# The first norm of a four-layer attention kernel: one tile's statistics and the root on ScalarE, masked queries taken from PSUM

## The chip, the cores and the metric

The kernel runs on one core of a Trainium2 chip. Five engines work side by side: TensorE (PE; PEld is its weight load), VectorE (DVE), ScalarE (ACT), GpSimd (POOL) and SyncE (SP), which issues the DMAs. The metric is the device time of one launch in microseconds, lower is better.

## The reference

Four layers work on one sequence of 2048 tokens with 512 features: A, B, A, B, with the same weights for both A layers and for both B layers. Cut to what matters:

```python
x = A_x                                                  # 1 x 2048 x 512, bf16
x = x + A(layernorm(x));  x = x + B(layernorm(x))
x = x + A(layernorm(x));  x = x + B(layernorm(x))

def layernorm(x):                                        # over the 512 features
    return (x - mean(x)) / sqrt(var(x) + 1e-5)

def A(x):       # 32 heads of 16, 4 segments of 512 tokens, one after the other
    q, k, v = heads(x @ wq), heads(x @ wk), heads(x @ wv)
    for s in segments:
        a_dot = softmax(q[s] @ k[s].T / 4 + causal_mask) @ v[s]     # inside the segment
        a_mem = phi(q[s]) @ M / (phi(q[s]) @ z + 1e-6)              # memory of earlier segments
        out[s] = g * a_mem + (1 - g) * a_dot                        # g = sigmoid(beta), per head
        M += phi(k[s]).T @ v[s];  z += sum(phi(k[s]))
    return out @ wo

def B(x): return softmax(q @ k.T / 4) @ v @ wo           # 32 heads over all 2048 tokens
```

## The kernel before

The program is written out once, at build time, by a planner in Python (`Builder`), and every engine then runs its own fixed list in order. The planner keeps an estimated time for each engine (the `ns` and `gap` arguments); it picks from a list of attention units and a list of background tasks (norm, projections, memory, output) and appends the instructions. What waits for what follows from the tiles that each instruction reads and writes, and is kept by semaphores: an instruction waits for the last writer of what it reads. Two rules matter here. A PSUM bank counts as one tile, and where two engines read the same bank, the later reader in the program also waits for the earlier one (`last_read_any` in `Sched.add`). And a bank that is to be written anew waits for all who read its old content.

**The attention unit.** Attention works in units of up to three banks of scores: three matmuls of 32 rows (one for each head of a group, from the masked queries `qm` and the keys `KA` or `KB`), one exponential on ScalarE over the three banks (L1349), and later the product with the values. The units use the banks 0 to 2 and 4 to 6 in turn, bank 3 (`DXB`) takes the background's matmuls once attention runs, and bank 7 (`ACC`) collects the product with the values. Queries are masked because a group holds every second head: `qm` is a copy of the 128 query rows in which the other heads' rows are multiplied by zero (`par` holds the mask; L1266, one instruction for each half of the heads).

**The start.** Everything before the first unit is one chain, and the change lies there:

- `setup` (L447 on) issues the loads on SP's queue: the first four tiles of x, one by one (128 tokens each), then the weights wk, wq, wv, beta, then the other twelve tiles of x in three loads, then wo, wqkv and wo of B. PE runs 66 matmuls on an identity meanwhile. DVE reduces the head mask to `par` and sets two PSUM banks, `ACC` and `DXB`, to zero (L490).
- `task_A` for layer 0, segment 0, calls `ln_part`: per tile `bn_stats` (L519) and `bn_aggr` (L521) on DVE, then 1 / sqrt(var + eps) for the four tiles at once by eight small instructions on DVE (L526 to L533: a first value from the bits of the number, and two Newton steps).
- `ln_first` normalizes the four tiles on DVE (L552), transposes them on PE (L406, 16 matmuls) into banks 3 and 0, and copies them to `xT`: the first half on ACT, the second on DVE (L564, L565).
- Then the projections of the first 128 features: keys into bank 1, copied to `KA` by DVE (L429), queries into bank 2, copied to `QA` by ACT (L427); DVE masks `QA` twice into `qm` (L1266); the first three score matmuls write banks 0 to 2; the projection of the values follows behind them in PE's list, and the first exponential waits for all three.

From there on, background and attention interleave to the end of the program.

## Time and profile before

| | before |
|---|---|
| median of 3 runs | 1893.77 us (1893.45 to 1894.54) |
| the profiled execution: own time | 1894.24 us |
| its span, first to last instruction | 1892.7 us |
| granted TensorE clock, mean | 0.994 |
| busy: PE, ACT, DVE, POOL | 89%, 95%, 81%, 15% of the span |
| first exponential of attention starts | 14.48 us |

The profiled execution took 1.54 us more than its span (what lies before the first and behind the last instruction), and 0.47 us more than the median of the runs. All times of the trace count from the first instruction of the span.

In the profile's rows a line number is that of the kernel's source; "out<-in" names the tiles; "xN" merges N instructions in a row on one engine, with the time that they cover together; the bracket tells how long the engine stood idle and what ended that.

### The profile page before, as it was taken

What the parts mean: (1) busy time and instruction counts of PE and PEld (TensorE: products, weight loads), DVE (VectorE), ACT (ScalarE), POOL (GpSimd) and SP (SyncE); (2) the same over time, 40 slices, a digit from 0 to 9 for tenths busy, and PEclk for the clock granted to TensorE, in tenths of its full rate; (3) what the DMA queues carried; (4) which work ended last, traced back from release to release, by engine and by line L of the source; (5) the groups of instructions that cost most, each with busy time, mean ns of one, the idle gap of its engine ahead of it and who ended that gap; (6) DMA issues with size and microseconds to landing.
All of it is one profiled execution on the core that took longest, in us unless ns stands there. A gap on an engine that the chain in (4) does not pass through costs nothing.

```text
span 1892.7 us, 64181 instructions
## 1 busy us (share of the span) xinstructions
PE 1686.8 (89%) x27966; PEld 891.0 (47%) x28200; DVE 1535.3 (81%) x3230; ACT 1798.6 (95%) x1642; POOL 277.7 (15%) x646
## 2 busy tenths in 40 slices
PE   7879888899998999999989989899888898889887
PEld 4444445566665556665656656555522222222222
DVE  6566657698797678797778779678999999999996
ACT  6899999899999999999999999999999999999998
POOL 4522333010001110001110050420100000000000
PEclk9999999999999999999999999999999999999999
DMA  5121110000000002000001011010100000000000
GB/s 159 29 35 38 24 18 19 14 14 17 14 8 9 8 8 31 12 19 8 9 8 33 11 24 25 19 19 3 14 12 1 1 11 2 2 1 13 1 1 12
DMA packets 94971, 33.51 MB, mean 18 GB/s; under 512 B 87521, under 2 KB 94177, under 8 KB 94689
## 3 DMA queue, kind: packets, MB, share of 16 engines
q1 hardware_dynamic: 94688, 29.39, 8.0%
q8 instruction: 221, 3.62, 0.8%
q14 instruction: 62, 0.50, 0.1%
HBM read 6.30 MB, written 2.10 MB: 4 GB/s over the span
## 4 chain that ended last, share of the span: by engine, by line
PE 40%; ACT 29%; DVE 16%; issue 12%; DMA 2%; POOL 1%; SPq 0%; ACTq 0%; DVEq 0%; POOLq 0%
PE ps L402 40%; ACT pT L1349 29%; DVE dxw L980 3%; DVE dxw L1032 2%; DMA xT<-xn 1%; DVE ob L1459 1%; DVE lnst L519 1%; DVE x L795 1%; POOL pT L1364 1%; DVE QA L980 0%; DVE rd L1447 0%; DVE VA L1032 0%; DVE wA L980 0%; DVE KB L980 0%; DVE QA L1032 0%
## 5 line engine op out<-in xcount | busy, mean ns | idle before, releaser
L1349 ACT ACTIVATE pT<-ps 128x1536 bf16<-128x1536 f32 (+3 forms) x1605 | 1771.4, 1249 | 70.4 <-PE ps L402 57.6
L402 PE MATMUL ps<-qm,KB 32*128 32x512 bf16 x3584 | 491.6, 386 | 79.5 <-ACT pT L1349 56.5
L1364 POOL TENSOR_SCALAR_AFFINE_SELECT pT<-pT 128x256 bf16<-128x256 bf16 (+2 forms) x529 | 212.8, 421 | 830.4 <-ACT pT L1349 821.0
L402 PEld LDWEIGHTS ps<-VB,pT 128*128 128x128 bf16 x7800 | 256.6, 96 | 162.2 <-issue 107.0
L402 PE MATMUL ps<-VB,pT 128*128 128x51 bf16 (+1 forms) x7800 | 321.9, 187 | 10.7 <-DVE ob L1459 5.5
L980 DVE TENSOR_SCALAR dxw<-ps 128x512 uint16<-128x512 f32 (+1 forms) x309 | 269.8, 876 | 48.9 <-PE ps L402 45.6
L402 PEld LDWEIGHTS ps<-qm,KB 32*128 32x128 bf16 x3584 | 122.2, 91 | 284.0 <-ACT pT L1349 195.2
L402 PE MATMUL ps<-VB,dxw 128*128 128x34 bf16 (+1 forms) x5112 | 212.9, 186 | 0.2 <-issue 0.2
L1032 DVE TENSOR_SCALAR dxw<-dxw 128x1024 uint16<-128x1024 uint16 (+1 forms) x401 | 164.5, 426 | 8.0 <-PE ps L402 5.3
L402 PEld LDWEIGHTS ps<-VB,dxw 128*128 128x128 bf16 x5112 | 167.6, 96 | 5.7 <-issue 3.6
L1266 POOL TENSOR_SCALAR qm<-QB,par 128x512 bf16<-128x512 bf16 x74 | 57.9, 785 | 688.9 <-PE ps L402 560.3
L402 PE MATMUL ps<-VA,pT 128*128 128x51 bf16 (+1 forms) x3036 | 126.7, 188 | 20.0 <-DVE ob L1459 12.6
L402 PEld LDWEIGHTS ps<-VA,pT 128*128 128x128 bf16 x3036 | 100.0, 96 | 77.9 <-POOL pT L1364 42.8
L402 PE MATMUL ps<-qm,KA 32*128 32x128 bf16 (+3 forms) x1024 | 106.1, 303 | 24.0 <-ACT pT L1349 16.1
L402 PE MATMUL ps<-pT,VB 128*17 128x512 bf16 x791 | 126.1, 384 | 1.5 <-DVE KA L1477 0.6
L402 PE MATMUL ps<-qm,QA 32*128 32x512 bf16 x512 | 89.6, 385 | 24.8 <-ACT pT L1349 21.7
L402 PE MATMUL ps<-dxw,VB 128*17 128x512 bf16 x313 | 86.4, 381 | 0.0
L402 PEld LDWEIGHTS ps<-qm,KA 32*128 32x128 bf16 x1024 | 30.5, 91 | 87.7 <-ACT pT L1349 60.9
L402 PE MATMUL ps<-xT,wB 128*128 128x512 bf16 x223 | 63.4, 388 | 5.2 <-issue 2.4
L402 PE MATMUL ps<-xT,wA 128*128 128x512 bf16 x217 | 59.6, 380 | 8.4 <-issue 3.5
L402 PEld LDWEIGHTS ps<-pT,VB 128*17 128x17 bf16 x791 | 29.8, 87 | 76.4 <-issue 66.6
L402 PE MATMUL ps<-wB,zero 128*128 128x512 bf16 x173 | 60.9, 392 | 3.6 <-issue 2.4
(293 smaller groups left out, 2378.8 us busy)
## 6 DMA issues: line engine op xcount, KB each, us to landing
out_dram<-x SPq DMA_DIRECT2D x8, 256.0 KB, 2.1
x<-in_A_x_dram SPq DMA_DIRECT2D x3, 512.0 KB, 9.6
wB<-in_B_wqkv_dram SPq DMA_DIRECT2D x1, 1536.0 KB, 11.8
xT<-xn SPq DMA_TRANSPOSE x60, 2.5
oT<-ob SPq DMA_TRANSPOSE x52, 2.4
x<-in_A_x_dram SPq DMA_DIRECT2D x4, 128.0 KB, 2.1
wA<-in_A_wk_dram SPq DMA_DIRECT2D x1, 512.0 KB, 5.3
wA<-in_A_wq_dram SPq DMA_DIRECT2D x1, 512.0 KB, 6.2
```

The costliest lines, as they stand in the source:

```text
L402: self.sc.add("pe", lambda e: e.matmul(out, lhsT, rhs, start=start, stop=stop, skip_group_check=True), reads=reads, banks=[(bank, "w", all ...
L519: self.op("dve", (lambda i, t: lambda e: e.bn_stats(st[:, k, i, 0:6], self.x[:, t, :]))(i, t), reads=[self.b_x[t]], writes=[bs], ns=690)
L795: self.op("dve", (lambda t, o: lambda e: e.tensor_tensor(self.x[:, t, :], self.x[:, t, :], o, ALU.add))(t, o), reads=[self.b_x[t]], writes ...
L980: self.sc.add("dve", lambda e: e.tensor_scalar(d, o, SCALE * LOG2E * 128, EXP_C, op0=ALU.mult, op1=ALU.add), writes=[w for j in range(k) f ...
L1032: self.op("dve", lambda e: e.tensor_scalar(o, w, d, None, op0=ALU.add), reads=self.b_dxw[b0][:len(ents)], writes=wr, ns=435 if len(ents) = ...
L1266: self.op(eng, (lambda m, q, col: lambda e: e.tensor_scalar(m, q, col, 0.0, op0=ALU.mult, op1=ALU.add))(m, q, col), reads=[bq, self.b_par] ...
L1349: self.sc.add("act", (lambda dst, src: lambda e: e.activation(dst, src, ACT.Exp, scale=SCALE))(dst, src), writes=self.b_pT[slot * 3 + i:sl ...
L1364: self.op("pool", (lambda blk, pat: lambda e: e.affine_select(blk, blk, pattern=pat, compare_op=ALU.is_ge, fill=0.0, base=0, channel_multi ...
L1459: self.op("dve", lambda e: e.tensor_tensor(ob, src[:, :, 0:16], rb, ALU.mult), reads=[br] + bsrc, writes=[self.b_ob[oi][g.e]], bank=bk, al ...
```

## The change

Six edits, all in what runs before the first exponential or is queued there:

- **Statistics.** For the first segment `ln_part` is replaced by `ln_start`. Tiles 0, 1 and 3 keep `bn_stats` and `bn_aggr` on DVE. Tile 2 goes to ACT: a Copy with an accumulated sum gives minus the scaled mean, a Square with that as its bias and an accumulated sum gives the variance; DVE turns the first into the mean with one small instruction.
- **Root.** ACT takes sqrt(var + eps) of the four tiles in one Sqrt, and DVE one reciprocal, in place of the eight small instructions. Sqrt and Exp belong to different activation tables; a one-element Exp behind the Sqrt brings the second table back. In ACT's list there are now three table loads: ahead of the Copy, ahead of the Sqrt, ahead of that Exp.
- **Memsets.** `DXB` is no longer zeroed, and `ACC` is zeroed behind the four normalizing instructions in DVE's list instead of ahead of the statistics.
- **Masked queries from PSUM.** `first_heads` projects the queries first (bank 1), then the keys (bank 2). DVE writes the first masked queries straight from PSUM; ACT copies the queries to `QA` behind it (same bank, so it waits for the mask). The second mask is still made from `QA`.
- **First keys apart.** DVE copies keys 0 to 127 from bank 2, ACT the other 384 behind that; the first score matmuls wait for the small copy alone as far as the keys go.
- **Loads.** wq is loaded ahead of wk, and the load of tiles 4 to 7 of x waits on SP until wq and wk have landed; the loads behind it in SP's queue (the rest of x, wo, wqkv, wo of B) stand behind that wait.

In the compiled lists PE's instructions are the same in number and kind and in the same order; the other engines' lists differ only in the instructions named here.

```diff
@@ setup
-        for a, b in [...]: ... writes=self.b_x[a:b])
+        ... writes=self.b_x[a:b], deps=[self.b_wA[i].last_write for i in (0, 1)] if a == 4 else [])
             if a == 3:
-                for i, nm in ((1, "A_wk"), (0, "A_wq"), (2, "A_wv")):
+                for i, nm in ((0, "A_wq"), (1, "A_wk"), (2, "A_wv")):
...
-        for bk in (ACC, DXB):
-            ...
-            self.op("dve", (lambda b: lambda e: e.memset(self.ps[:, b.col0:b.col0 + 512], 0.0))(b), bank=b, alloc=-1)
+        pool(lambda e: e.memset(self.eps[:, :], LN_EPS), [self.b_eps])
@@ new
+    def ln_start(self):
+        junk, root = self.pT[:, 0, 0, :], 512 ** 0.5
+        for i in (0, 1, 3):
+            ... bn_stats, bn_aggr of x[:, i, :] on dve
+        nb = st[:, k, 2, 0:1]
+        self.op("act", lambda e: e.activation(junk, self.x[:, 2, :], ACT.Copy, scale=-1 / (512 * root), accum_out=nb), ...)
+        self.op("act", lambda e: e.activation(junk, self.x[:, 2, :], ACT.Square, scale=1 / root, bias=nb, accum_out=st[:, k, 2, 7:8]), ...)
+        self.op("dve", lambda e: e.tensor_scalar(st[:, k, 2, 6:7], nb, -root, None, op0=ALU.mult), ...)
+        self.op("act", lambda e: e.activation(v, var, ACT.Sqrt, bias=self.eps[:, 0:1]), ...)
+        self.op("act", lambda e: e.activation(self.eps[:, 1:2], self.eps[:, 0:1], ACT.Exp), ...)
+        self.op("dve", lambda e: e.reciprocal(y, v), ...)
@@ ln_first, behind the four normalizing instructions
+        self.op("dve", lambda e: e.memset(self.ps[:, b.col0:b.col0 + 512], 0.0), bank=b, alloc=-1)     # ACC
@@ new, in place of proj_fm of keys and queries for layer 0, segment 0, c = 0
+    def first_heads(self, slot):
+        for i, dst in ((0, self.QA), (1, self.KA)):
+            bank, al = self.misc(), self.new_alloc()
+            ... four matmuls into the bank
+            if i:
+                dve: tensor_copy(d[:, 0:128], o[:, 0:128]), writes b_K0
+                act: activation(d[:, 128:512], o[:, 128:512], ACT.Copy), reads b_K0
+            else:
+                dve: tensor_scalar(qm[:, 0, :], o, par[:, 0:1], 0.0, op0=ALU.mult, op1=ALU.add)
+                act: activation(d, o, ACT.Copy)
@@ select
+                if (g.L, g.qseg, g.c, g.e) == (0, 0, 0, 0):
+                    self.sel.append(g)
+                    continue                       # its mask was made in first_heads
@@ unit
-                kt = lambda kb: (..., self.b_KA[sl][g.c])
+                kt = lambda kb: (..., self.b_K0 if (g.L, g.qseg, g.c, kb) == (0, 0, 0, 0) else self.b_KA[sl][g.c])
```

More of the change, by code (lines that the diff above doesn't have):

```diff
@@ L314, in alloc @@
         self.lnw = sb("lnw", [P, 2, 4, 4], f32)
+        self.eps, self.b_eps = sb("eps", [P, 2], f32), Buf("eps")
+        self.b_K0 = Buf("k0")
         self.bet = sb("bet", [P, H], bf)
@@ L534, in ln_part @@
         return k
+    def ln_start(self):
+        k = self.ring("ln", 2)
+        st, w = self.lnst, self.lnw
+        bs = self.b_lnst[k]
+        junk, root = self.pT[:, 0, 0, :], 512 ** 0.5
+        yield [], 0, 3000
+        for i in (0, 1, 3):
+            self.op("dve", (lambda i: lambda e: e.bn_stats(st[:, k, i, 0:6], self.x[:, i, :]))(i), reads=[self.b_x[i]], writes=[bs[i]], ns=690)
+            self.op("dve", (lambda i: lambda e: e.bn_aggr(st[:, k, i, 6:8], st[:, k, i, 0:6]))(i), reads=[bs[i]], writes=[bs[i]], ns=180)
+        nb = st[:, k, 2, 0:1]
+        self.op("act", lambda e: e.activation(junk, self.x[:, 2, :], ACT.Copy, scale=-1 / (512 * root), accum_out=nb),
+                reads=[self.b_x[2]], writes=[bs[2], self.b_pT[0]], ns=620, gap=500)
+        self.op("act", lambda e: e.activation(junk, self.x[:, 2, :], ACT.Square, scale=1 / root, bias=nb, accum_out=st[:, k, 2, 7:8]),
+                reads=[self.b_x[2], bs[2]], writes=[bs[2], self.b_pT[0]], ns=620, gap=500)
+        bw = self.b_lnw[k]
+        v, y, var = w[:, k, 0, :], w[:, k, 1, :], st[:, k, :, 7]
+        self.op("dve", lambda e: e.tensor_scalar(st[:, k, 2, 6:7], nb, -root, None, op0=ALU.mult), reads=[bs[2]], writes=[bs[2]], ns=165)
+        self.op("act", lambda e: e.activation(v, var, ACT.Sqrt, bias=self.eps[:, 0:1]), reads=bs + [self.b_eps], writes=[bw], ns=230, gap=150)
+        self.op("act", lambda e: e.activation(self.eps[:, 1:2], self.eps[:, 0:1], ACT.Exp), reads=[self.b_eps], writes=[self.b_eps], ns=1500,
+                gap=1400)
+        self.op("dve", lambda e: e.reciprocal(y, v), reads=[bw], writes=[bw], ns=165)
+        return k
     def normalize(self, s, k, i):
@@ L554, in ln_first @@
                     reads=[self.b_x[t], self.b_lnst[k][t], self.b_lnw[k]], writes=[bx])
+        b = self.banks[ACC]
+        b.alloc = -1
+        self.op("dve", lambda e: e.memset(self.ps[:, b.col0:b.col0 + 512], 0.0), bank=b, alloc=-1)
         for j in range(2):
@@ L625, in task_A @@
         yield need, 0, 0
-        k = yield from self.ln_part(L, s)
+        k = yield from (self.ln_part(L, s) if L or s else self.ln_start())
         yield ["xT"], 0, 0
@@ L1308, in unit @@
                 sl = self.aslot(g.L, g.qseg)
-                kt = lambda kb: (self.KA[rows, sl, g.c, kb * 128:(kb + 1) * 128], self.b_KA[sl][g.c])
+                kt = lambda kb: (self.KA[rows, sl, g.c, kb * 128:(kb + 1) * 128], self.b_K0 if (g.L, g.qseg, g.c, kb) == (0, 0, 0, 0) else self.b_KA[sl][g.c])
                 parts = PARTS[what]
```

30 lines of the change are left out of this document (23 added, 7 removed).

## The prediction

> **What bounds the kernel now.** I read the page's busy shares first, then the chain of waits over the stretch that the change touches, then the timeline of that stretch, and last the rows that give prices. Over the whole program ScalarE is the fullest engine:
>
> ```profile
> PE 1686.8 (89%) x27966; PEld 891.0 (47%) x28200; DVE 1535.3 (81%) x3230; ACT 1798.6 (95%) x1642; POOL 277.7 (15%) x646
> ```
>
> That average says nothing of the first 14 us, where ScalarE does almost nothing. What counts there is the chain (start, us, what), here from the end of the head mask to the first exponential:
>
> ```profile
> by line: DVE lnst L519 19.5%; PE ps L402 17.4%; PE ps L406 11.6%; issue 8.3%; DVE ps L490 8.2%; DVE lnst L521 6.2%; DVE xT L565 5.9%; ACT QA L427 5.1%; DVE xn L552 3.5%; DVE qm L1266 3.1%; DVE lnw L532 2.9%; DVE lnw L531 2.9%; DVE lnw L533
> ```
>
> Memsets (L490), statistics (L519, L521) and root (lnw) all stand on the path, and so do the query copy and the mask. No DMA does. So what is saved here moves the first exponential, and with it everything behind it, as long as nothing later hangs on an absolute time. The timeline gives the places (start, length, engine, instruction):
>
> ```profile
> 0.80 1.82 SPq L449 DMA_DIRECT2D x<-in_A_x_dram  x4
> 0.80 1.28 ACT L564 ACT_TABLE_LOAD   x1 [0.80 <-PEq L1697]
> 2.57 1.03 DVE L490 MEMSET ps<- 128x512 f32 x2
> 3.50 0.64 DVE L519 BATCH_NORM_STATS2 lnst<-x 128x6 f32<-128x512 bf16 x1
> ...
> 5.86 0.66 DVE L519 BATCH_NORM_STATS2 lnst<-x 128x6 f32<-128x512 bf16 x1
> 6.56 0.18 DVE L521 BATCH_NORM_AGGREGATE lnst<-lnst 128x2 f32<-128x6 f32 x1
> 6.77 0.17 DVE L526 TENSOR_SCALAR lnw<-lnst 128x4 f32<-128x4 f32 x1
> ...
> 8.17 0.16 DVE L533 SCALAR_TENSOR_TENSOR lnw<-lnw 128x4 f32<-128x4 f32 x1
> 8.37 0.73 DVE L552 TENSOR_SCALAR xn<-x,lnst,lnw 128x512 bf16<-128x512 bf16 x2
> 9.02 0.73 DVE L552 TENSOR_SCALAR oT<-x,lnst,lnw 128x512 bf16<-128x512 bf16 x2
> 9.59 1.02 ACT L564 ACTIVATE xT<-ps 128x1024 bf16<-128x1024 bf16 x1 [7.51 <-PE ps L406]
> 10.24 0.69 DVE L565 COPY xT<-ps 128x1024 bf16<-128x1024 bf16 x1 [0.49 <-PE ps L406]
> 12.14 0.69 DVE L429 CAST KA<-ps 128x512 bf16<-128x512 f32 x1 [1.21 <-PE ps L402]
> 13.00 0.60 ACT L427 ACTIVATE QA<-ps 128x512 bf16<-128x512 f32 x1 [2.39 <-PE ps L402]
> 13.63 0.62 DVE L1266 TENSOR_SCALAR qm<-QA,par 128x512 bf16<-128x512 bf16 x2 [0.80 <-ACT QA L427]
> 14.04 0.39 PE L402 MATMUL ps<-qm,KA 32*128 32x512 bf16 x3 [1.08 <-DVE qm L1266]
> 14.36 1.04 PE L402 MATMUL ps<-wA,xT 128*128 128x512 bf16 x4
> 14.48 2.79 ACT L1349 ACTIVATE pT<-ps 128x1536 bf16<-128x1536 f32 x2 [0.88 <-PE ps L402]
> 17.16 0.23 ACT L496 ACTIVATE gtok<-bet 128x32 f32<-128x32 bf16 x1
> 17.27 0.23 ACT L496 ACTIVATE gout<-bet 128x32 f32<-128x32 bf16 x1
> ```
>
> To be seen: DVE works without a break from 2.57 to the end of the normalizing at 9.75, the eight root instructions alone take 6.77 to 8.33, and three places count: normalizing starts at 8.37, the transposed x is whole at 10.93, the score matmuls start at 14.04, which is 3.11 behind 10.93.
>
> Rows for prices, from the page (landing of a load behind its issue, median) and from the groups (count, busy, mean ns):
>
> ```profile
> x<-in_A_x_dram SPq DMA_DIRECT2D x4, 128.0 KB, 2.1
> wA<-in_A_wk_dram SPq DMA_DIRECT2D x1, 512.0 KB, 5.3
> wA<-in_A_wq_dram SPq DMA_DIRECT2D x1, 512.0 KB, 6.2
> ```
>
> ```profile
> L1349 ACT ACTIVATE pT<-ps 128x512 bf16<-128x512 f32 x91 | 50.7, 671 | 4.8 <-PE ps L402 3.5 <-POOL pT L1364 0.8
> L1349 ACT ACTIVATE pT<-ps 128x256 bf16<-128x256 f32 x48 | 19.8, 412 | 0.1
> L1435 DVE COPY KB<-ps 128x272 f32<-128x272 f32 x8 | 3.4, 430 | 0.5 <-PE ps L402 0.5
> L1447 DVE RECIPROCAL rd<-ps 128x16 f32<-128x16 f32 x88 | 22.0, 250 | 42.9 <-PE ps L402 42.3
> ```
>
> **Part 1: statistics and root, to the start of normalizing.** Without the memsets DVE waits for the first tile, issued at 0.80 and landed 2.1 later, at 2.90. Its three tiles then take 0.79 each (5.86 against 3.50 is three steps) and end at about 2.95 + 3 x 0.79 = 5.3. That is not what comes last. ScalarE's branch does: the third tile is issued 0.93 behind the first (four issues cover 1.82), so at 1.73, and lands at 3.83, work begins at about 3.90. Copy 0.60 (the QA row, same size); reading out the sum is not in the trace, I take the shortest ScalarE instruction, 0.23, in full, since the next step waits for it; hand-over 0.03; Square 0.60; read-out 0.23; table load 1.28 with 0.04 around it; Sqrt 0.23; hand-over 0.03; reciprocal 0.20 (between the 0.17 of a four-element DVE instruction and the 0.25 of L1447); hand-over 0.03. Sum 3.50, so normalizing starts at 7.40 against 8.37: **0.97 gained**. The small mean instruction on DVE waits for the Square and lies beside the table load. Bounds: with free read-outs (0.46 less) and a 0.17 reciprocal the gain is 1.46; with 0.67 for each 512-wide pass (the L1349 row) and a 0.35 reciprocal it is 0.68.
>
> The Trainium skill, "ScalarE: Activation LUTs", section "What ACT_TABLE_LOAD costs", adds about 93 ns for a per-partition pointer operand, which the Square and the Sqrt each carry as a bias. By it the sum of part 1 would be about 0.78; no row of this trace shows such an operand on ScalarE.
>
> **Part 2: from normalizing to the transposed x.** The same instructions, plus the `ACC` memset, 0.49 (two in 1.03), that now stands between the normalizing and DVE's half of the copy. In the trace DVE idles exactly 0.49 there, waiting for PE. So it fits with nothing to spare, and costs 0.05, between 0 and 0.10. ScalarE's half must be free for the other half: behind the Sqrt, which ends 0.26 before normalizing starts, come a table load and the small Exp, 1.28 + 0.02 + 0.23, so it is free 1.27 behind the start of normalizing, and PE's first half is ready 1.22 behind it (9.59 against 8.37). Its copy ends 1.27 + 1.02 = 2.29 behind, DVE's half 2.56 + 0.05. The second table load is hidden by 0.3 and costs nothing. The transposed x is whole at 10.93 - 0.97 + 0.05 = 10.01.
>
> **Part 3: from there (X) to the score matmuls.** The queries are in PSUM at X + 1.21 (12.14 against 10.93). DVE's mask from PSUM costs what such a pass costs, 0.69: X + 1.90. ScalarE's copy of the queries reads the same bank and waits for it: X + 1.93 to X + 2.53. The keys are in PSUM at X + 2.07 (13.00); DVE's 128 columns cost 0.32 (between 0.25 for 16 and 0.43 for 272): X + 2.40. The first score matmul can start there, 0.7 earlier than now. But the three write banks 0, 1 and 2, which now hold nothing, queries, keys. The second waits for ScalarE's query copy, the third for ScalarE's copy of the other 384 key columns, which stands behind the query copy in ScalarE's list. It costs 0.51 (between 0.41 for 256 and 0.60 for 512) and overlaps its forerunner by 0.11 (the two gate rows, 0.23 long and 0.12 apart): X + 2.42 to X + 2.95, and the third matmul starts at X + 3.00 against X + 3.11. The first exponential needs all three, and the value projection stands behind the third in PE's list. So masking from PSUM and the split copy together give **0.1**, not 0.7: ScalarE's two copies in a row are late next. Bounds: 0, without the overlap, and 0.15.
>
> **Part 4: loads.** wq, now first, lands where wk did, 2.67 + 5.3 = 7.97, wk where wq did, 3.15 + 6.2 = 9.35. Queries start at X + 0.1 = 10.1 and keys 0.86 later: neither waits. Behind SP's new wait stand the other x loads and wo, wqkv, wo of B, some 9.4 instead of 4.80. Their first readers are late enough:
>
> ```profile
> 4.80 3.88 SPq L449 DMA_DIRECT2D x<-in_A_x_dram  x3
> wB<-in_B_wqkv_dram SPq DMA_DIRECT2D x1, 1536.0 KB, 11.8
> 30.13 0.68 DVE L519 BATCH_NORM_STATS2 lnst<-x 128x6 f32<-128x512 bf16 x1
> L402 PEld LDWEIGHTS ps<-wB,zero x28: 94/96/98, 39.6 to 124.3; 128*128 128x128 bf16 x28
> ```
>
> Tile 4 is read at 30.13, wqkv of B at 39.6 (first of the group; landed at 10.21 + 11.8 = 22.0 now). A delay of all these by 4.6 us would still be hidden by 12 us or more. Cost nothing.
>
> **Sum.** 0.97 - 0.05 + 0.1 = 1.0 us. The rest of the program is the same lists, moved by that much. The profiled execution, 1894.24, would become 1893.2; it stands 0.47 over the median, so the median becomes 1893.77 - 1.0 = **1892.8**. Its own range: gain 0.5 to 1.6 (all bounds together), and the runs before lie from 0.3 under to 0.8 over their median, so 1891.8 to 1894.1.
>
> **Rivals.** *A, the table loads cost more than their row, and it gets slower.* The one load of before runs at 0.80 with nothing behind it until 9.59, so the trace cannot show what a load does to a busy ScalarE. If each holds the engine for a time d on top of the 1.28, normalizing starts at 7.40 + d, and ScalarE's half of the transposed x ends at 7.40 - 0.26 + d + 1.28 + d + 0.25 + 1.02 = 9.7 + 2d, later than DVE's half (10.0 + d) once d passes 0.3. Beyond d = 0.66 the start is later than now. With d as long as the load itself, 1.28: 9.7 + 2.56 = 12.26, 1.33 late, less 0.1: +1.2 us, 1895.0. For it: two switches stand on the path, where there was none. Against it: nothing in the trace drains or blocks besides the row. The same section of the Trainium skill speaks against this change: a switch of sets costs a load of about 1283 ns, as in this trace, and a drain of about 1380 ns besides, 2.66 us in all. By that rule the sum would be +1.4 us instead of -1.0; no row here shows the drain.
>
> *B, the gain is swallowed.* A shift of 1 us could be taken up by a later wait on something that did not move, or the ScalarE branch could be slower than its bounds. Then 1893.8. Against it: the only things tied to absolute time are the loads, with 12 us of slack.
>
> *C and D, the clock.* Five stretches run at half the clock; the first and the last of the five by windows (length, PE, PEld, DVE, ACT, POOL busy, granted clock, ...):
>
> ```profile
> 360.00:368.00 8.00, 6.91 (x43) 3.08 (x45) 2.00 (x4) 1.95 (x3) 0.69 (x1) 0.57 0.00 0
> 981.00:985.50 4.50, 3.44 (x61) 2.62 (x63) 3.34 (x8) 2.75 (x3) 0.00 (x0) 0.62 0.16 33
> ```
>
> The first loses at most 8.0 x 0.43 = 3.4 us of PE work, the last 4.5 x 0.38 = 1.7. If the new phase brings one more of each, +5.1 - 1.0: 1897.9 (C); if it spares one of each, 1887.7 (D). It decides from about three half-clock pieces on. Against both: the runs shown lie within 1.1 us, less than one piece. The Trainium skill, "TensorE: Matmul & The Clock Gate", section on the clock gate in Part 1, says that the window by which the clock is judged runs freely and does not restart with a kernel. By that rule the runs of before have sampled the phases already.
>
> **How the numbers follow.** Chances: the forecast 0.70, A 0.12, B 0.08, C and D 0.05 each. Without A the range would leave out 0.22, so it reaches up to A's 1895.0 and 0.2 beyond, for d a tenth longer than the load: 1891.8 to 1895.2, with C and D left out. About 0.2%, 3.8 us, is what a measurement of this kernel can tell from no change. The forecast, A and B all lie inside that: 0.90 within; D gives 0.05 faster, C 0.05 slower.
>
> **What would show it.** Right: no memset ahead of the first `bn_stats`, which starts near 2.95; normalizing at 7.4; the transposed x whole near 10.0; the first score matmul near 12.4 but the third near 13.0, behind ScalarE's key copy; the first exponential near 13.5; from there the rows of before, 1.0 earlier. Wrong: an idle stretch of ScalarE beside its second and third table load and ScalarE's half of the copy ending last (A); the read-outs longer than 0.23; the third matmul as early as the first, which would make the gain 1.6; a later idle stretch that ends at the old time (B); another number of half-clock stretches (C, D).

## The result and the profile after

| | before | after |
|---|---|---|
| median of 10 runs each | 1894.37 us (1893.45 to 1897.93) | 1899.05 us (1896.24 to 1904.12) |
| ratio after / before | | 1.0024, 95% interval 1.0014 to 1.0034 |
| profiled execution: own time, span | 1894.24, 1892.7 us | 1900.96, 1899.2 us |
| its granted clock | 0.994 | 0.989 |
| first exponential | 14.48 us | 13.47 us |

Forecast was 1892.8. The kernel came out slower by 4.7 us in this comparison, although the start did what the forecast said. Both numbers need one remark: the time of a launch depends on where the clock's windows happen to fall in it, and these ten runs of before lie low. In the 136 later runs of before that came with a granted clock the median is 1896.7 (1890.6 to 1903.8). Over all 277 timed runs with their clocks (the two kernels with more filling, below, apart) one slope fits, with a level of its own for each kernel: 1.32 us for each 0.001 of mean granted clock, 1.15 us of scatter beside it. "At equal clock" below is the difference to the runs of before that were taken on the same chip at the same time, after that line is taken off, with its 95% interval (before itself differs by up to 1.2 us between such groups). Expectations that speak of the same granted clock use an earlier figure, over all groups at once, which is 0.2 to 0.8 higher. The changed kernel stands **1.5 +- 0.8 us above before at equal clock** (12 runs; all 23 runs of it against all 136 of before, over all groups, 1.9 +- 0.5), and not 1.0 below.

The busy shares of after are those of before:

```profile
PE 1693.5 (89%) x27966; PEld 894.1 (47%) x28200; DVE 1530.9 (81%) x3221; ACT 1804.9 (95%) x1651; POOL 277.7 (15%) x647
```

The timeline of after from the first statistics to the first exponential (start, length, engine, line, what; the bracket is the idle time ahead):

```profile
2.98 0.69 DVE L544 BATCH_NORM_STATS2 lnst<-x 128x6 f32<-128x512 bf16 x1 [0.51 <-DMA x<-in_A_x_dram]
3.97 0.63 ACT L547 ACTIVATE pT<-x 128x512 bf16<-128x512 bf16 x1 [1.89 <-DMA x<-in_A_x_dram]
4.51 0.19 ACT L547 ACTIVATION_READ_ACCUMULATOR pT<-x 128x1 f32 x1
4.73 0.72 ACT L549 ACTIVATE pT<-x,lnst 128x512 bf16<-128x512 bf16 x1
5.36 0.19 ACT L549 ACTIVATION_READ_ACCUMULATOR pT<-x,lnst 128x1 f32 x1
5.56 1.28 ACT L554 ACT_TABLE_LOAD   x1
6.85 0.30 ACT L554 ACTIVATE lnw<-lnst,eps 128x4 f32<-128x4 f32 x1
7.17 1.28 ACT L555 ACT_TABLE_LOAD   x1
7.19 0.18 DVE L557 RECIPROCAL lnw<-lnw 128x4 f32<-128x4 f32 x1 [1.27 <-ACT lnw L554]
7.40 0.74 DVE L576 TENSOR_SCALAR xn<-x,lnst,lnw 128x512 bf16<-128x512 bf16 x2
8.46 0.20 ACT L555 ACTIVATE eps<-eps 128x1 f32<-128x1 f32 x1
8.63 1.02 ACT L591 ACTIVATE xT<-ps 128x1024 bf16<-128x1024 bf16 x1
8.89 0.48 DVE L581 MEMSET ps<- 128x512 f32 x1
9.28 0.68 DVE L592 COPY xT<-ps 128x1024 bf16<-128x1024 bf16 x1
12.02 0.60 ACT L695 ACTIVATE QA<-ps 128x512 bf16<-128x512 f32 x1 [2.37 <-PE ps L404]
12.04 0.29 DVE L688 CAST KA<-ps 128x128 bf16<-128x128 f32 x1
12.38 1.05 PE L404 MATMUL ps<-qm,KA 32*128 32x512 bf16 x3 [0.39 <-DVE KA L688]
12.51 0.48 ACT L689 ACTIVATE KA<-ps 128x384 bf16<-128x384 f32 x1
13.05 0.09 PEld L404 LDWEIGHTS ps<-qm,KA 32*128 32x128 bf16 x1 [0.29 <-ACT KA L689]
13.47 1.45 ACT L1404 ACTIVATE pT<-ps 128x1536 bf16<-128x1536 f32 x1 [0.48 <-PE ps L404]
```

Normalizing starts at 7.40, as forecast; the transposed x is whole at 9.96 (forecast 10.01); the third score matmul starts at 13.05 (forecast 13.0) behind ScalarE's key copy; the first exponential is 1.01 earlier than before. That is one launch: in the two further profiles of the changed kernel ScalarE's Copy starts at 3.88 and 4.37, behind a load that lands sooner or later, normalizing at 7.31 and 7.80, and the first exponential at 13.38 and 13.88, while in all three profiles of before it starts at 14.48. The start gains 0.6 to 1.1 us. Whatever made the kernel slower lies behind it.

### The profile page after: what moved, and what is told of

Read it like the earlier page. It is cut to its first block, busy times and chain, and to the rows that moved or that the text cites. A ratio compares the mean times of both kernels' runs of the same rounds, so it can differ in the third digit from the quotient of the medians.

```text
span 1899.2 us, 64185 instructions
## 1 busy us (share of the span) xinstructions
PE 1693.5 (89%) x27966; PEld 894.1 (47%) x28200; DVE 1530.9 (81%) x3221; ACT 1804.9 (95%) x1651; POOL 277.7 (15%) x647
## 4 chain that ended last, share of the span: by engine, by line
PE 39%; ACT 30%; DVE 15%; issue 12%; DMA 2%; POOL 1%; SPq 0%; ACTq 0%; DVEq 0%
PE ps L404 39%; ACT pT L1404 30%; DVE dxw L1031 3%; DVE dxw L1083 2%; DMA xT<-xn 1%; DVE ob L1514 1%; DVE lnst L518 1%; POOL pT L1419 1%; DVE x L846 0%; DVE rd L1502 0%; DVE QA L1031 0%; DMA oT<-ob 0%; DVE VA L1083 0%; ACT amem L631 0%; DVE xn L565 0%
```

## The experiments

**The same two programs again.** One more profiled launch of each; nothing is edited.

> The kernel before, unchanged, for a second profile. Theory W (the windows by which the clock is judged lie the same way in every launch, and the changed kernel meets them 1 us earlier): the half-clock stretches lie at 360, 531, 637, 808 and 982 us again, within 1 us, and the time is 1893.5 to 1894.5. Theory F (the windows lie at random to each launch): half-clock stretches at partly other places, their grid of 3.41 us moved, time 1893.5 to 1898. Theory L (something in the changed lists of instructions lowers PE's activity for good) says nothing on this run beyond 1893.5 to 1898.

> The changed kernel, unchanged, for a second profile. Theory W: half-clock stretches again at 28, 93, 219, 584, 635, 813, 980, 1086, 1113 and 1212 us, time 1900 to 1901.5. Theory F: other places, time anywhere from 1896 to 1904. Theory L: a core of places that come back in every launch whatever the grid, above all the early ones at 28 and 93 us, and the rest changing; time 1896 to 1904.

Before took 1899.7 us with 14 half-clock pieces (each 3.413 us long), after took 1894.88 with 7: the order of the first comparison, turned round. Both programs get more or fewer such pieces from launch to launch, 7 to 14 in the six profiles of the two unedited kernels. One way in which a piece comes about is seen in two windows laid on the pieces' grid, first in the first profile of after, then in that of before (window, length, PE, PEld, DVE, ACT, POOL busy, granted clock, DMA share, GB/s):

```profile
24.44:27.85 3.41, 1.35 (x29) 0.88 (x31) 1.69 (x5) 1.95 (x4) 2.05 (x5) 1.00 0.00 0
27.85:31.26 3.41, 3.41 (x27) 1.27 (x24) 2.24 (x5) 2.73 (x2) 0.73 (x2) 0.50 0.02 5
```

```profile
22.59:26.00 3.41, 2.60 (x35) 1.27 (x33) 1.92 (x4) 2.69 (x3) 1.61 (x4) 1.00 0.01 2
26.00:29.42 3.42, 1.87 (x31) 0.97 (x34) 1.19 (x4) 1.96 (x4) 1.61 (x5) 1.00 0.02 5
```

In after the stretch in which PE has little to do falls into one window, PE is busy for 1.35 of 3.41 us in it, and the next window runs at half clock. In before the same stretch is cut by the grid into windows with 2.60 and 1.87, and no half clock follows. Busy time alone does not decide it, though: the windows ahead of the other pieces of these two profiles (the one at the very end apart) had PE busy for 1.0 to 2.5 us, most of them for longer than that 1.87. The grid stood at another offset to the span's start in each profile: 2.1 us in the first of before, 0.54 in after, 0.40, 0.68, 2.67, 1.32 and so on in those that followed. That agrees with the Trainium skill, "TensorE: Matmul & The Clock Gate", Part 1, by which the window runs freely and does not restart with a kernel.

**The start moved by a fixed amount.** Two memsets more on DVE ahead of the normalizing, in both kernels:

```diff
+        for i in range(2):
+            self.op("dve", ... e.memset(self.dxw[:, i, :], 0.0), writes=self.b_dxw[i], ns=0, gap=0)
```

> The changed kernel with two extra DVE memsets of an unused tile right ahead of the normalizing, so that everything from the first normalizing on comes about 1 us later, at the places that it had in the kernel before; all other lists are the same. Theory W: the kernel before's windows are met again, five half-clock stretches, 1893.8 to 1895. Theory L: 1 us more than the changed kernel, about 1900. Theory F: also 1900, since a shift means nothing to a grid at random.

> The kernel before with the same two extra memsets, so everything from the first normalizing on comes about 1 us later. Counting PE's streamed columns of the profile before by windows of 3.41 us, nine windows lie under the level at its own grid and eleven with the grid moved by 1 us. Theory W: 1 us of shift and two more half-clock pieces at 1 to 1.7 us each, 1897 to 1899. Theories F and L: the shift alone, 1895.4.

After with them: 1896.93, ratio 1.0006 (0.9992 to 1.0021), first exponential at 14.22, at equal clock +1.4 +- 0.7 us. Before with them: 1900.51, ratio 1.0017 (1.0002 to 1.0032), at equal clock +1.3 +- 0.7. The theories had their times from single launches, and none of them gave either of these. With the grid at another offset in every profile theory W is out, and so the loss does not come with the phase of the start. The edit of the changed kernel is not a shift alone, however: it also puts two entries into DVE's list, and three exponentials that come late in the unedited changed kernel (numbers 609, 941 and 1400, looked at below) start 1.60, 1.52 and 1.67 us behind their predecessors here, close to before. A later start and a repair are mixed in this run; that it measures no worse than the changed kernel does not say that 0.75 us at the start is worth nothing.

**More launches of each.** Unedited again, 12 runs.

> The changed kernel, unchanged, in many more runs. Theory G (the grid of the clock's windows lies at random to each launch, the number of half-clock pieces changes from launch to launch between 7 and 14 in both kernels, and apart from these the changed kernel is within half a microsecond of the one before: 1.0 won at the start, 0.65 and 0.2 lost at places that come back in every profile of it): mean and median within 1.2 us of the kernel before's, whose 19 runs lay from 1892.5 to 1900.9 around 1896.35, so 1895 to 1897.5; mean clock 0.990 to 0.991. Theory P (the changed kernel meets more half-clock pieces for good): 1898.5 to 1900 and a mean clock lower by 0.001 or more.

> The kernel before against itself: what a comparison of two equal programs gives here. Theory G: the same spread as in its earlier 19 runs, 1892.5 to 1901, and a ratio of medians that can be off by 0.1% in either direction though nothing differs. Theory P: the same, it says nothing on this run.

After: 1897.03, ratio 1.0017 (1.0003 to 1.0031), at equal clock +1.5 +- 0.8. Before against itself: 1897.82, ratio 1.0005 (0.9991 to 1.0020), at equal clock -0.1 +- 0.7. The mean granted clock over all runs is 0.9905 for after and 0.9903 for before, so the change does not bring more half-clock pieces: the forecast's case C is out and theory P with it. Theory G's half a microsecond is too little, too: something else costs after its 1.5 us.

**More filling against the half clock.** The planner sets fill matmuls on `zero` into PE's gaps; here it may set more:

```diff
-    FILL, FILLS = 0.5, 2
+    FILL, FILLS = 0.55, 3
```

> The changed kernel with the planner's two constants for filler matmuls raised from 0.5 and 2 to 0.55 and 3, so 432 fillers instead of 259: more of PE's poor stretches are kept above the level at which the clock is halved. Its lists differ from those of the next kernel only in the instructions of the change. Theory G: fewer half-clock pieces (at most 6), a spread of the runs under 4 us instead of 8, and a time within 0.7 us of the next kernel's. Theory P: 2 us or more above the next kernel, by more half-clock pieces, or as much as that with as few pieces if the loss isn't the clock's.

> The kernel before with the same two constants. Theory G: at most 6 half-clock pieces, spread under 4 us, mean clock 0.994 or more; the time 1890 to 1897, depending on what the 173 extra fillers (0.22 us of PE each, 37 us in all) hold up. Theory P: the same.

319 fill matmuls in place of 173. Four pieces in after and seven in before, clock 0.996 and 0.994, and yet 1907.3 and 1910.91 us, ratios 1.0063 (1.0044 to 1.0081) and 1.0082 (1.0062 to 1.0102), from four runs each. The two lie 3.6 us apart, the changed kernel below, which neither theory said. With these constants the planner writes another program throughout (1601 exponentials in place of 1605, VectorE's lists 22 entries shorter), so this is the price of the setting, not of the fill matmuls alone, and the pair says nothing of the change. By this setting the half clock is cheaper than what would keep it away.

**VectorE's list at its old length.** The change took nine entries out of DVE's list (3608 to 3599, semaphore entries counted). Comparing the exponentials' starts one by one over the profiles of each kernel, the largest loss that no half-clock piece explained was at exponential 941 (the first of all is number 0), where a DMA transpose came late. Nine one-element memsets behind the copy of the transposed x give the list its old length:

```diff
+        for i in range(9):
+            self.op("dve", ... e.memset(self.dxw[0:1, i, 0:2], 0.0), writes=self.b_dxw[i], ns=0, gap=0)
```

> The changed kernel with nine one-element DVE memsets without waits put behind DVE's half of the first transposed x, where DVE idles for 1.2 us: DVE's list then has as many entries as in the kernel before, and from there on every DVE instruction has its old place in the list. Taking all runs of the two kernels so far against their granted clocks, the changed kernel is 1.9 us slower at the same clock (at 0.991: 1897.6 against 1895.7). Theory I (instruction fetching: DVE's next 128 entries are fetched by a DMA of 8 KB; the change made DVE's list nine entries shorter, so one of these fetches now falls between two transposing DMAs near 1103 us, which then land in 4.0 to 4.6 us instead of 3.3, and DVE and the three products behind them come 0.7 to 1.7 us late): those transposes land as in the kernel before, the wait there goes, and at clock 0.991 the time is 1895.5 to 1896.5. Theory C (the clock's pieces merely fall at dearer places in the changed kernel): 1897.6 at 0.991, as without the padding. The first exponential starts at 13.4 to 13.9 by both.

1896.77, ratio 0.9993 (0.9979 to 1.0006), at equal clock 0.0 +- 0.7, where the changed kernel had +1.5 +- 0.8. Exponential 941 starts 1.20 behind its predecessor (in the unedited profiles of before 0.89 to 1.44, of after 2.24 to 2.59), 609 starts 1.60 behind (1.60; 2.25 to 2.44), 1400 starts 1.67 behind (1.67; 2.02). What happens at 941 is in the DMA view of 7 us ahead of 941 (queue: packets, MB, share of 16 engines; issues with median us to landing; then the wait of DVE), for before, after and the padded kernel:

```profile
q1 hardware_dynamic: 1632, 0.39, 32.1%
oT<-ob SPq DMA_TRANSPOSE x1, 3.4
  DMA oT<-ob: 0.8, 1
```

```profile
q1 hardware_dynamic: 1632, 0.39, 49.7%
q14 instruction: 1, 0.01, 1.5%
oT<-ob SPq DMA_TRANSPOSE x1, 4.7
  DMA oT<-ob: 2.2, 1
```

```profile
q1 hardware_dynamic: 1632, 0.39, 31.9%
oT<-ob SPq DMA_TRANSPOSE x1, 3.6
  DMA oT<-ob: 1.1, 1
```

The same 1632 packets take 49.7% of the engines' time instead of 32.1% when one transfer of the queue named `instruction` falls between them (it moves 0.50 MB in 61 transfers over the program, some 8 KB each). In three other profiles in which the transfer falls elsewhere or later (two of kernels with DVE's old list, and the one with two memsets), these packets take 30% to 40%, and the transpose lands after 3.6 to 4.0 us. In after the transpose lands after 4.7 us, DVE waits 2.2 us for it, and the scores and the exponential behind it wait too:

```profile
1107.39 4.69 ACT L1404 ACTIVATE pT<-ps 128x1536 bf16<-128x1536 f32 x5
1113.47 1.45 ACT L1404 ACTIVATE pT<-ps 128x1536 bf16<-128x1536 f32 x1 [1.39 <-PE ps L404]
```

This transfer comes at a fixed place of DVE's list, near its entry 2110 in all profiles. With nine entries fewer, entry 2110 is reached five exponentials later (behind 937 of them instead of 932), and that is between these two transposes. At 609 it is again a late transpose: PE waits 0.59 us there for `xT` in the second profile of after, and not at all in the second of before. At 1400 no transpose runs. There VectorE itself pauses, in after and not in before, ahead of the instruction that is entry 3136 of its list (3136 is 64 and a multiple of 128, a place that matters for ScalarE below, too). What this instruction waits for, PE among it, was there 0.4 us earlier:

```profile
1648.51 0.69 DVE L1031 TENSOR_SCALAR phq<-ps 128x512 uint16<-128x512 f32 x1
1649.64 0.43 DVE L1083 TENSOR_SCALAR VB<-VB 128x1024 uint16<-128x1024 uint16 x1 [0.44 <-PE ps L404]
```

```profile
1642.55 0.69 DVE L980 TENSOR_SCALAR phq<-ps 128x512 uint16<-128x512 f32 x1
1643.33 0.43 DVE L1032 TENSOR_SCALAR VB<-VB 128x1024 uint16<-128x1024 uint16 x1
```

In stretches that no half-clock piece disturbs, the 25 exponentials from 600 on take 0.7 us longer with the nine entries missing (29.3 to 29.9 us, otherwise 28.6 to 28.9), and the 25 from 1380 on 0.35 (29.61, otherwise 29.26). For the 30 from 930 on, compared where each has one half-clock piece, it is about 0.9 (32.6 to 32.9, otherwise 31.7 to 32.0). That is 2.0 us together.

**Other banks.** The padded kernel, and the first queries and keys in banks 4 and 5 instead of 1 and 2, which the first scores need:

```diff
-            bank, al = self.misc(), self.new_alloc()
+            self.misc()
+            bank, al = self.banks[4 + i], self.new_alloc()
```

> As the run with the padded list, and the first queries and keys are projected into banks 4 and 5 instead of 1 and 2, so that the second and third score matmul no longer wait for ScalarE's two copies. If these waits are what keeps the masked queries and the split key copy from paying (part 3 of the prediction), all three score matmuls start together behind DVE's key copy, 0.6 us earlier than the third does now (12.4 instead of 13.05), and the first exponential starts when ScalarE is through with its key copy, 0.4 to 0.5 earlier, at 13.0 (13.4 in a launch with a late warm-up). If something else holds the exponential, it stays at 13.4 to 13.9. Time at the same clock: 0.4 to 0.5 less than with the padded list alone; the second unit, which writes banks 4 to 6, must not wait for the copies.

> The kernel with the padding and the other banks once more, as the comparison for the first of this call: before -0.3 at the same clock (first time -0.4 +- 0.7), all eleven exponentials slow. If it comes out 1 us faster than the first time, the gain of one Copy more in the earlier call was spread between calls and not the Copy.

The first time 1896.75, ratio 0.9995 (0.9982 to 1.0007); the second 1894.53, ratio 0.9989 (0.9975 to 1.0003); at equal clock -1.2 +- 0.7 both times; the 2 us between the two medians are the half clock and the group. The three score matmuls now run in a row (timeline of the second), and the exponential no longer waits for PE. It follows ScalarE's copy of the keys, which runs from 12.65 to 13.13, without a break:

```profile
12.52 0.10 PEld L404 LDWEIGHTS ps<-qm,KA 32*128 32x128 bf16 x3 [0.88 <-DVE KA L691]
12.52 0.39 PE L404 MATMUL ps<-qm,KA 32*128 32x512 bf16 x3 [0.39 <-DVE KA L691]
13.02 1.46 ACT L1407 ACTIVATE pT<-ps 128x1536 bf16<-128x1536 f32 x1
```

The first exponential starts 2.92 behind the transposed x, not 3.51. These 0.6 us are most of the 0.7 which the forecast's third part said was blocked by ScalarE's two copies.

**The third part alone.** The kernel before with `first_heads` and wq loaded first; norm, memsets and the other loads as they were:

```diff
+            if (L, s, c) == (0, 0, 0):
+                self.first_heads(slot)
```

> The kernel before with the masked queries from PSUM, the split key copy and wq loaded ahead of wk alone; statistics, root, memsets and the other loads as before. By part 3 of the prediction the third score matmul starts 3.00 to 3.10 behind the transposed x, against 3.11, and the first exponential at 14.37, 0.1 earlier than in the kernel before (bounds 14.33 and 14.48). If the mask from PSUM paid in full it would be 13.8. The time is a single run, 1890 to 1901, and tells nothing of this.

> The kernel before with the first masked queries from PSUM, the first keys apart and wq loaded first; norm, memsets and the other loads as before. ScalarE's list is 3 longer, VectorE's as long as before. The forecast's third part gives a first exponential 0.1 earlier (14.4 beside 14.48 where the clock is full at the start). Theory of the lists: stalls at other exponentials than in the changed kernel and about as many (3 more is odd, as 11 is), none at 941: before +0.3 to +0.6 at the same clock. Rival (the start alone decides): before -0.1.

The single launch (1894.24) tells nothing of the start: it met a half-clock piece at 11 us, and the first exponential came at 15.76. Over 12 runs: 1896.84, ratio 1.0001 (0.9987 to 1.0015), at equal clock +0.9 +- 0.9, first exponential at 14.45 against 14.48, behind these rows:

```profile
13.35 1.06 PE L404 MATMUL ps<-qm,KA 32*128 32x512 bf16 x3 [0.39 <-DVE KA L688]
14.45 1.45 ACT L1404 ACTIVATE pT<-ps 128x1536 bf16<-128x1536 f32 x1 [0.48 <-PE ps L404]
```

So this part gives 0.03, where the forecast said 0.1, and no more. At equal clock the kernel is rather slower than before, which is the side of the theory of the lists: exponentials 284 and 1438, now entries 576 and 2880 of ScalarE's list, start 0.28 us later behind their predecessors than in before (1.33 and 1.30, not 1.05 and 1.02), and 941 is as in before (1.45). The size is not settled by this interval.

**ScalarE's list made longer in the kernel before.** The change puts 11 entries into ScalarE's list (3215 to 3226). Eleven exponentials stand out: in all profiles of after they start later behind their predecessors than in any of before. Ten of them do so by 0.16 to 0.28 us, although nothing they waited for was late, and these ten are entries 448, 832, 1472 and so on of ScalarE's list, semaphore entries counted: 64 and a multiple of 128. The eleventh, 1057, is entry 2126 and no such place; most of its difference comes from a pause that before has shortly ahead of it, at 1055, entry 2112, and that after has not. Before has such a pause at 795, entry 1600, too. The kernel before with 11 one-element copies at the head of ScalarE's list:

```diff
+        for i in range(11):
+            self.op("act", ... e.activation(self.dxw[0:1, ...], self.par[0:1, 0:1], ACT.Copy), reads=[self.b_par], ns=0, gap=0)
```

> The kernel before with eleven one-element ScalarE copies in its idle time ahead of the first transposed x: ScalarE's list is longer by eleven entries, as in the changed kernel, and nothing else differs. Theory S (ScalarE stalls 0.27 us at every 64th entry of its list, counted from the same point in both kernels, wherever the entry there has no slack): the exponentials number 214, 724, 983, 1306 and 1434 (counted from the first) come 0.27 us later behind their forerunners than in all four profiles of the kernel before, as in all profiles of the changed kernel; number 795 comes 0.27 earlier. Rival: these differences come from the changed kernel's data placement or its activation tables, then none of them appears. First exponential 14.48 in both cases; time a single run, 1890 to 1901.

The ten stalls appeared, each at its place, the one at 795 went (1.08 behind its predecessor, not 1.37), and 1057 moved as in after. The expectations count every 64th entry. The profiles show less: in all of them, ScalarE's instructions at entries 64, 192, 320 and on in steps of 128 start up to 0.34 us behind the last thing that they waited for, those at every other place of the list, multiples of 128 among them, at most 0.06. A transfer of the queue `instruction` starts within 1.3 us of each of these 25 entries in the first profile of after. Exponential 1306 in the timelines of before, of after and of this kernel:

```profile
1536.50 5.21 ACT L1349 ACTIVATE pT<-ps 128x1536 bf16<-128x1536 f32 x4
```

```profile
1543.34 2.42 ACT L1404 ACTIVATE pT<-ps 128x1024 bf16<-128x1024 f32 x2
1546.03 2.37 ACT L1404 ACTIVATE pT<-ps 128x1536 bf16<-128x1536 f32 x2 [0.28 <-ACT pT L1404]
```

```profile
1545.80 3.77 ACT L1352 ACTIVATE pT<-ps 128x1536 bf16<-128x1536 f32 x3
1549.85 1.45 ACT L1352 ACTIVATE pT<-ps 128x1536 bf16<-128x1536 f32 x1 [0.27 <-ACT pT L1352]
```

Before runs four exponentials in a row without a break; the other two break by 0.28 and 0.27 us ahead of 1306, and what the engine "waited for" is its own predecessor. (This launch took 1904.04 us with 15 half-clock pieces; one run prices nothing.)

**The same undone in the changed kernel.** One one-element Copy more at the head of ScalarE's list, with the padding and the other banks, and alone:

```diff
+        self.op("act", lambda e: e.activation(self.eps[:, 1:2], self.eps[:, 0:1], ACT.Copy), reads=[self.b_eps], writes=[self.b_eps], ns=0, gap=0)
         nb = st[:, k, 2, 0:1]
```

> The changed kernel with the nine padding entries on DVE, the first queries and keys in banks 4 and 5, and one one-element Copy more at the head of ScalarE's list, so that this list is 12 entries longer than before the change and not 11. Theory (ScalarE stalls 0.27 us at every 64th entry of its list): at 11 more, 40 of the 48 such places in the rest of the program are exponentials or copies, at 12 more 37 of 48 are semaphore entries that wait beside a running exponential; the stalls at exponentials 214, 406, 724, 1049, 1057, 1178, 1306, 1370, 1434, 1562 go (1306 starts 1.52 behind its predecessor, not 1.79; 406 0.92, not 1.14), and at the same granted clock the time is 0.6 to 0.9 below that of the kernel with the other banks: before -1.2, median 1895.5 or so beside before's 1896.8. Rival (the stalls come from waits that the change brings, not from the place in the list): they stay where they are, and the time is that of the kernel with the other banks, before -0.4.

> The changed kernel with that one Copy more at the head of ScalarE's list and nothing else. Theory: the ten stalls go as above, the slow DMA transposes at exponential 941 (increments over 2) stay, since VectorE's list is as it was; at the same granted clock before +1.0 (the changed kernel stood at before +1.7). Rival: both stay, before +1.7.

This missed its aim: the Copy took over a wait for GpSimd that had needed a semaphore entry of its own, and the list stayed 3226 long. All eleven exponentials stayed late too, as they must if the place decides. 1894.82 and 1898.14, ratios 0.9989 (0.9976 to 1.0001) and 1.0015 (1.0003 to 1.0026), at equal clock -1.1 +- 1.0 and +1.3 +- 0.8, which is what the same kernels have without the Copy (-1.2 and +1.5). Then two Copies (3227 entries):

```diff
+        for i in range(2):
+            self.op("act", lambda e: e.activation(self.eps[:, 1:2], self.eps[:, 0:1], ACT.Copy), reads=[self.b_eps], writes=[self.b_eps], ns=0, gap=0)
```

> As the kernel with the other banks and one Copy more, but with two. The one Copy took a semaphore entry away with it (the table load no longer waits for GpSimd), so the list stayed 11 longer than before the change; two make it 12 (3227 entries). Theory (the place in the list): exponentials 214, 406, 724, 983, 1049, 1057, 1178, 1306, 1370, 1434, 1562 return to 0.51, 0.92, 0.54, 1.51, 0.69, 0.93, 0.90, 1.52, 0.90, 0.91, 0.90; a few others (435, 661, 886) may lengthen by 0.27; at the same granted clock 0.4 to 0.7 below the other banks of this call. Rival (waits that the change brings): they stay at 0.78, 1.14, 0.81, 1.80 and so on, and so does the time.

> The changed kernel with the same two Copies and nothing else. Theory: the eleven return as above, 609, 941 and 1400 stay slow (2.25, over 2, 2.02); before +1.0 to +1.3 at the same clock. Rival: nothing moves, before +1.8.

In both, ten of the eleven went back to the value of before: 214 from 0.78 to 0.50, 406 from 1.14 to 0.92, 724 from 0.81 to 0.53, 1306 from 1.79 to 1.51, and so on; only 1057, which stands at no such place, stayed longer (1.20, before 0.93). A new pause came at 661, now entry 1344 (1.27, before 0.99); none came at 435 and 886. The timeline of the first at 1306:

```profile
1537.80 6.13 ACT L1409 ACTIVATE pT<-ps 128x1536 bf16<-128x1536 f32 x5
```

Five in a row, no break. In the second the late exponentials 609, 941 and 1400 stayed (2.24, 2.18, 2.01), since DVE's list was left short there. Of the stalls, those at 983, 1049, 1178, 1306 and 1370 are not made good within the next twenty units; by those rows the two Copies are worth 0.28 + 0.20 + 0.17 + 0.27 + 0.18 = 1.1 us. From that comes off 0.3: the twenty exponentials from 720 on take 18.54 us with the two Copies, as in before, and 18.24 with the pause at 724, so a pause can also shorten what follows. The times can only say that this is not contradicted: 1894.50, ratio 0.9989 (0.9975 to 1.0004), at equal clock -1.9 +- 0.5, beside -1.2 +- 0.7 for the other banks in the same group; and 1898.17, ratio 1.0017 (1.0004 to 1.0030), +1.1 +- 0.9, where the changed kernel had +1.5 +- 0.8.

The kernel with padding, other banks and two Copies is the lowest of the study at equal clock, and below before; its interval overlaps that of the other banks alone, and by the plain ratio it still touches 1.

## Why the prediction was wrong

**Parts 1 and 2 were right.** Sum of part 1: forecast 7.40, measured 7.40. Its terms: the Copy took 0.63 and not 0.60, the Square 0.72 and not 0.60, the Sqrt 0.30 and not 0.23, the read-outs 0.19 and not 0.23, and the Copy started at 3.97 and not 3.90; against that, each read-out starts 0.09 before the end of its pass. The errors cancelled, and the hit to the hundredth is luck: in the other two profiles of the kernel normalizing starts at 7.31 and 7.80. The Trainium skill, "ScalarE: Activation LUTs", section "What ACT_TABLE_LOAD costs", has about 93 ns for each pointer operand; the Square's 0.09 over the Copy agrees. In part 2 the memset cost 0.01, inside the stated 0 to 0.10, and ScalarE's half was ready first.

**Rival A fell.** The two table loads take 1.28 each, and the next instruction starts 0.01 behind the end of each (6.85, 8.46). The drain of about 1380 ns, which the same section adds to a change of sets, does not show in any profile here.

**Part 3 was right in its main point** (the third matmul at 13.05 behind ScalarE's second copy, so nothing like 0.7), with 0.03 to 0.04 in place of 0.1 for the first exponential: it starts 3.51 behind the transposed x where before it was 3.55, and the mask from PSUM took 0.75 and not 0.69. That the sum of 1.0 came out at the first exponential even so is because part 2 cost less by as much. The other banks show that the copies named were what held it, for 0.6. **Part 4** was right: the other loads were issued from 8.44 on, earlier than the 9.4 assumed, and no instruction waited for them.

**The step that failed is in the sum: "The rest of the program is the same lists, moved by that much."** They are not the same lists. DVE's was nine entries shorter and ScalarE's eleven longer, and two costs, which the prediction put at nothing, hang on the place of an instruction in its list. The first is DVE's: a transfer of the queue `instruction` that now met two transposes at 941, a late transpose at 609 and a pause of VectorE at 1400, 2.0 us by their rows. Padding the list took them away, and the equal-clock difference went from +1.5 +- 0.8 to 0.0 +- 0.7. The second is ScalarE's stalls at every 128th entry, shown in both directions, by lengthening the old list and by shifting the new one. Before has such stalls at other exponentials, so only the balance counts: 1.1 us at the five stalls that are not made good and 0.14 in the twenty exponentials from 860 on, less 0.31 and 0.23 that the twenty from 720 and from 780 on are shorter, 0.7 us. No time alone shows this second cost. About 0.2 us more behind the last exponential (9.08 against 8.88, in all kernels with the new norm; the last engine's work ends equally late behind it in both) and 0.2 outside the span (1.72 to 1.82 against 1.55 to 1.65) were not explained. An estimate from these rows is 2.0 + 0.7 + 0.4 - 1.0 = 2.1 us above before, and 1.5 +- 0.8, or 1.9 +- 0.5 over all runs, was measured. For the padded kernel with the other banks the same rows give about 0.3 below before, where 1.2 +- 0.7 below was measured, so the account is not complete. Rival B, the gain swallowed later, named the right side, but its reason against, "the only things tied to absolute time are the loads", left out the loading of the program itself, which the page counts in its third part. B's size (nothing gained) was too small as well.

**The second failure is the range.** That "the runs shown lie within 1.1 us" stood against C and D. Four runs had not sampled the phases: over 136 runs before spreads over 13 us. The grid of the windows did lie at another offset in each launch; the inference that the runs shown had sampled it was wrong. Of the 4.7 us in the first comparison about 3 are this scatter: the ten runs of before had a median 2.4 below that of the later ones.

## What to carry to other kernels

An edit at the start of a long unrolled program shifts every later instruction in its engine's list, and where an engine has no slack that alone can cost more than the edit brings: count the entries that an edit adds to each list (semaphore entries too), and vary the length by a few one-element instructions before judging it. Before a gain below one half-clock piece is claimed or denied, time the unchanged kernel against itself over dozens of launches, and compare at equal granted clock. And when a wait is taken off the path, look which bank or engine the next operation still shares with the one that was late: here two other banks gave 0.6 us that masking from PSUM alone did not.

## What the runs showed that was not expected

- ScalarE pauses for up to 0.34 us ahead of every 128th entry of its list (64, 192, 320, ...), where that entry is an exponential without slack; where a semaphore entry stands there, it passes beside a running exponential. Of the 24 such places from entry 192 on, 20 are ScalarE operations at 11 entries more than before, 7 in before and 5 at 12 more.
- A transfer of some 8 KB on the instruction queue in the middle of two DMA transposes went with a landing of 4.7 us in place of 3.4 and a share of the same packets of 50% in place of 32%. That the pauses of ScalarE and VectorE are their own instruction loading is an inference from the spacing and from the transfers that start beside them; no row names it as what the engine waits for.
- A window of 3.413 us in which PE was busy for 1.35 us was followed by one at clock 0.50; windows with 1.87 and 2.60 were not, but one with 2.50 elsewhere was, so busy time is not the measure. One piece more or less is worth some 1.2 us here (1.32 us for each 0.001 of mean clock, 1893 us long).
- A plan with 319 fill matmuls in place of 173 brought the profiled clock to 0.996 and 0.994 and cost 12 and 15 us.
